# Splitting the second product around the first one, with the two row tiles exchanging PSUM banks

## The chip, the core and the metric

The kernel runs on one core of a Trainium2 chip. The metric is the device time of one execution in microseconds (us); lower is better. The engines are TensorE (PE in the profile; its weight loads are shown apart as PEld), VectorE (DVE), ScalarE (ACT), GpSimd (POOL) and SyncE (SP, which issues DMAs). They run side by side and meet through semaphores.

## The reference, cut to what matters

```python
def sm(a, b):
    s = scale * (a @ b.transpose(0, 2, 1))
    s = s - s.max(-1, keepdims=True)
    e = np.exp(s)
    return e / (e.sum(-1, keepdims=True) + 1e-09)
x = sm(q, agents) @ (sm(agents, k) @ v)      # q, k, v: (2, 12480, 128), agents: (2, 49, 128)
x = x.reshape(24960, 128)
h = x @ w_in                                 # 128 -> 2048
g = np.maximum(h, 0.0) + alpha * np.minimum(h, 0.0)
out = g @ w_out                              # 2048 -> 128
```

## The kernel before

The kernel first does the agent attention of batch 0 and folds the result with `w_in` into a table `sab` of 49 agents x 2048 features. After that a main loop runs over 24,960 tokens. It takes them in 52 groups of 480 (`GT`), and each group in 8 steps (`NM`) of 256 features: 416 steps. Two groups share one softmax of the queries, so what else happens in the loop repeats every 16 steps, 26 times. The agent attention of batch 1 (`kb`, `v`, `e`, `kl`, `av` in the names) is done in pieces between the steps of batch 0.

Values are split into a high and a low part to keep precision, so each product is three matmul jobs: low x high, high x low, high x high.

A **first product** `g1(s)` gives `h`, 256 features of 480 tokens, from the query softmax `qmh`, `qml` and `sab`. 49 agents fit into 64 rows, so the PE array is used as two row tiles of 64 rows: the upper tile computes one block of 128 features, the lower tile the other, and each writes a PSUM bank of its own. That is three pairs of matmuls. ScalarE then writes `rh`, the high part of max(h, 0), and VectorE writes `rl`, the rest. `h` has two buffers, so `g1(s + 2)` may start only when `rh` and `rl` of step `s` have been taken from `h`.

A **second product** `g2(s)` multiplies `rh` and `rl` with the two parts of `w_out` (`wh`, `wl`, scaled by 1 - alpha) and adds into `acc`. Here each block of 128 features is cut into its upper and lower 64 rows; the upper row tile adds into bank 0 of `acc`, the lower into bank 1. Six jobs of two matmuls are six pairs: four that need `rh` alone, and then two that need `rl`. After the eighth step three more matmuls add the linear part of the activation (`zh`, `zl`), one on the upper tile and two on the lower; ScalarE and VectorE add the two banks into `os`, and the result is transposed, scaled and stored.

The order of work is written out: instructions of an engine stand in the order in which the Python code issues them, and a planner (`at`, `pre`, `fit`, `hold`) places the other work in the steps. One step issues: the work in `first` (copies of earlier results out of PSUM), `g1(s + 2)`, the planned work of the step (some of it matmuls: `lg`, `qsum`, `kl`, `av`), and `g2(s)`. The other groups of PSUM (`pair_tile`) take turns with `acc`. The functions that the change touches:

Of the kernel before, what the change touches and what calls it, by code (L numbers as in the profile page):

```python
# [31 lines left out]
def kernel(  # L32
# [11 lines left out]
    nc = tc.nc  # L44
# [7 lines left out]
    GT = 480  # L52
# [10 lines left out]
    NM = NF // 2  # L63
# [14 lines left out]
    TILES = ((0, HALF), (HALF, P))  # L78
# [3 lines left out]
    def pair_tile(name, i=None):  # L82

        i = (step[0] // NM + 1) % 2 if i is None else i
        return late[i].tile([P, 2, 512], F32, tag="x", name=name)
# [22 lines left out]
    wh = const.tile([P, NF, D], F32R, name="wh")  # L108
    wl = const.tile([P, NF, D], F32R, name="wl")
# [684 lines left out]
    hh, rr, oo = {}, {}, {}  # L794
# [17 lines left out]
        )  # L812
        rr[s] = (rh, rl)

    def g2(s):
        g, m = divmod(s, NM)
        w = st[g // NG]
        if m == 0:
            oo[g] = pair_tile(f"acc{g}", g % 2)
        acc = oo[g]  # L820
        rh, rl = rr.pop(s)
        jobs = [(wl, rh, 0), (wh, rh, 0), (wl, rh, 1), (wh, rh, 1), (wh, rl, 0), (wh, rl, 1)]
        for n, (a, x, u) in enumerate(jobs):
            for i, (r0, r1) in enumerate(TILES):
                nc.tensor.matmul(  # L825
                    acc[:, i, 0:GT], lhsT=a[r0:r1, 2 * m + u, :], rhs=x[r0:r1, u, :],
                    start=m == 0 and n == 0, stop=False,
                )
        if m == NM - 1:
            mh, ml = gq.pop(("M", g))  # L830
            for i, a, x in ((0, "zh", mh), (1, "zl", mh), (1, "zh", ml)):
                r0, r1 = TILES[i]
                nc.tensor.matmul(  # L833
                    acc[:, i, 0:GT], lhsT=w[a][r0:r1, :], rhs=x[r0:r1, :],
                    start=False, stop=x is ml or i == 0,
                )
            t = p1m.tile([P, GT], F32, tag="os", name=f"os{g}")
            nc.scalar.copy(out=t, in_=acc[:, 0, 0:GT])  # L838
            nc.vector.tensor_tensor(out=t, in0=acc[:, 1, 0:GT], in1=t, op=ALU.add)  # L839
            oo[g] = t  # L840
# [28 lines left out]
    with tc.manual_schedule():  # L869
# [30 lines left out]
        s = 0  # L900
        for c, (lo, hi) in enumerate(spans):
# [4 lines left out]
            s = max(s, hi + 5)  # L906
# [18 lines left out]
        for n in range(8):  # L925
            load, ops = (load_win, narrow_win) if n < 4 else (load_wo, narrow_wo)
            s = int(SLAB_FIRST + n * SLAB_STEP)
# [59 lines left out]
        def fit(s, **costs):  # L987

            while any(load.get((e, s), 0.0) + c > ROOM[e] for e, c in costs.items()):
                s += 1  # L990
            for e, c in costs.items():
                use(s, e, c)
            return s
# [3 lines left out]
        def hold(s):  # L997

            while s in busy or s + 1 in busy or s % NM in (0, 1, NM - 1):
                s += 1  # L1000
            busy.update((s, s + 1))
            return s
# [28 lines left out]
        for b in range(1, B):  # L1031
# [4 lines left out]
            s = base + 9  # L1036
            done, used = {}, {}
            for c, (lo, hi) in enumerate([*parts[:-1], (NU - 3, NU - 1), (NU - 1, NU)]):
                us = tuple(range(lo, hi))
                for u in us:  # L1040
                    s = fit(max(s, done.get(u - 3, 0) + 1), dve=0.57)
# [12 lines left out]
            s = t_max + 1  # L1054
# [3 lines left out]
            for lo, hi in parts:  # L1058
                us = list(range(lo, hi))
                t_av = s  # L1060
                for u in us:
                    s = fit(s, dve=0.3)
# [16 lines left out]
            s = t_av + 2  # L1079
# [3 lines left out]
            for f in lead:  # L1083
                s = hold(s)
                at(s, f)
                s += 2
            s = hold(s)
# [5 lines left out]
        for s in range(NS):  # L1093
            step[0] = s
            for f, a in first.pop(s, ()):
                f(*a)
            if s + 2 < NS:
                g1(s + 2)
            for f, a in plan.pop(s, ()):
                f(*a)  # L1100
            g2(s)
        for s in sorted(plan):
            for f, a in plan[s]:
                f(*a)
# [30 lines left out]
```

## Time and profile before

| | |
|---|---|
| median of 3 runs | 1071.53 us (1068.31 to 1077.67) |
| the profiled execution: its own time | 1069.83 us |
| its span in the trace | 1068.0 us |
| PE busy, of the span | 1027.9 us, 96% |
| VectorE busy | 821.9 us, 77% |
| ScalarE busy | 629.5 us, 59% |

The profile is of one execution. Its span is what the trace covers; 1.8 us of the execution's time lie outside it. A line number such as L803 is that of the kernel's file. Matmul rows overlap: a row begins when the matmul begins, and its duration holds a tail in which the next one already runs, so the pace of PE is read from the distance between starts.

### The profile page before, as it was taken

The page shows a single profiled execution, that of the slowest core. Times are in us where ns is not written, and L with a number is a line of the kernel's source. Part 1 is how long each engine was busy: PE and PEld are TensorE (multiplying, and loading weights), DVE is VectorE, ACT ScalarE, POOL GpSimd, SP SyncE. Part 2 cuts the span into 40 slices and gives each one's busy share as a digit, 9 for nine tenths or more (in the row PEclk, how much of TensorE's full clock was granted, in tenths as well). Part 3 has the DMA queues.
Part 4 walks back from the last instruction along what each step waited for, and adds up shares of the span by engine and source line. Part 5 has one row for each costly group of instructions (what it writes and reads, how often), then busy time and mean ns, then how long its engine had stood idle before and what let it go on. Part 6 is the DMA issues. An engine that isn't in the chain of part 4 may idle for free.

```text
span 1068.0 us, 22363 instructions
## 1 busy us (share of the span) xinstructions
PE 1027.9 (96%) x9252; PEld 918.1 (86%) x9252; DVE 821.9 (77%) x1057; ACT 629.5 (59%) x805; POOL 111.7 (10%) x138
## 2 busy tenths in 40 slices
PE   7978999999999999999999999999999999999997
PEld 6865888888888888888877899998999989989997
DVE  6776588778778799989767777787778777786775
ACT  4454456556556577777555666566556665665553
POOL 3231110110110110110011011101110111001100
PEclk9889999999999999999999999999999999999999
DMA  8943041432331233233021022111211021202011
GB/s 295 287 96 49 4 76 30 68 60 37 61 59 28 55 71 77 69 79 62 11 39 30 16 33 38 30 20 29 37 30 33 16 38 30 39 11 38 11 20 29
DMA packets 295046, 57.23 MB, mean 54 GB/s; under 512 B 265567, under 2 KB 292769, under 8 KB 294945
## 3 DMA queue, kind: packets, MB, share of 16 engines
q1 hardware_dynamic: 293953, 55.69, 25.9%
q8 instruction: 72, 1.18, 0.5%
q14 instruction: 29, 0.24, 0.1%
q10 hardware_dynamic: 992, 0.12, 0.1%
HBM read 42.59 MB, written 12.78 MB: 52 GB/s over the span
## 4 chain that ended last, share of the span: by engine, by line
PE 63%; DVE 19%; ACT 12%; issue 4%; DMA 1%; SPq 0%; DVEq 0%; ACTq 0%
PE acc L825 33%; PE h L803 19%; DVE rl L810 8%; ACT rh L809 5%; PE lg L722 3%; ACT qs L749 3%; ACT qmh L744 3%; PE kl L379 2%; DVE qs L740 2%; PE av L567 1%; ACT os L838 1%; DVE qml L753 1%; DVE mx L418 1%; PE av L534 1%; DVE ql L712 1%
## 5 line engine op out<-in xcount | busy, mean ns | idle before, releaser
L810 DVE SCALAR_TENSOR_TENSOR rl<-h,rh 128x960 fp32r<-128x960 f32 x416 | 476.1, 1151 | 193.9 <-ACT rh L809 191.4
L809 ACT ACTIVATE rh<-h 128x960 fp32r<-128x960 f32 x416 | 402.4, 973 | 318.0 <-PE h L803 305.4
L803 PE MATMUL h<-qmh,sab 64*128 64x480 f32 x1664 | 378.0, 384 | 13.4 <-DVE rl L810 12.0
L825 PE MATMUL acc<-rh,wl 64*128 64x480 f32 x1664 | 374.8, 380 | 0.0
L825 PE MATMUL acc<-rh,wh 64*128 64x480 f32 x1664 | 371.9, 377 | 0.0
L825 PE MATMUL acc<-rl,wh 64*128 64x480 f32 x1664 | 294.2, 378 | 0.0
L803 PEld LDWEIGHTS h<-qmh,sab 64*128 64x128 f32 x1664 | 216.7, 184 | 49.5 <-DVE rl L810 32.6
L825 PEld LDWEIGHTS acc<-rh,wl 64*128 64x128 f32 x1664 | 217.8, 184 | 17.2 <-issue 3.4
L825 PEld LDWEIGHTS acc<-rh,wh 64*128 64x128 f32 x1664 | 218.3, 184 | 12.8
L825 PEld LDWEIGHTS acc<-rl,wh 64*128 64x128 f32 x1664 | 200.1, 184 | 14.2
L803 PE MATMUL h<-qml,sab 64*128 64x480 f32 x832 | 200.8, 378 | 0.0
L735 POOL PARTITION_ALL_REDUCE qm<-qs x26 | 79.2, 3045 | 761.0 <-ACT qs L730 694.3
L803 PEld LDWEIGHTS h<-qml,sab 64*128 64x128 f32 x832 | 111.5, 185 | 5.6
L379 PEld LDWEIGHTS kl<-ag,kt 64*128 64x128 f32 (+2 forms) x588 | 49.2, 192 | 2.6 <-issue 0.7
L379 PE MATMUL kl<-ag,kt 64*128 64x49 f32 (+2 forms) x588 | 50.0, 272 | 0.2 <-ACT kt L351 0.2
L839 DVE TENSOR_TENSOR os<-acc,os 128x480 f32<-128x480 f32 x52 | 33.6, 647 | 19.9 <-ACT os L838 19.8
L838 ACT COPY os<-acc 128x480 f32<-128x480 f32 x52 | 28.7, 551 | 23.3 <-PE acc L833 23.3
L707 ACT CAST qh<-qt 128x960 fp32r<-128x960 f32 x26 | 25.9, 998 | 16.1 <-DVE qt L700 16.1
L844 DVE STREAM_TRANSPOSE ot<-os 128x480 f32<-128x480 f32 x52 | 34.0, 653 | 0.0
L849 DVE TENSOR_TENSOR ot<-ot,qr 128x480 f32<-128x480 f32 x52 | 33.7, 648 | 0.1
L744 ACT ACTIVATE qmh<-qs,padb 128x960 fp32r<-128x960 f32 x26 | 28.5, 1098 | 7.7 <-DVE qs L740 7.7
L730 ACT COPY qs<-lg 128x960 f32<-128x960 f32 x26 | 25.0, 960 | 13.6 <-PE lg L722 13.6
(143 smaller groups left out, 856.6 us busy)
## 6 DMA issues: line engine op xcount, KB each, us to landing
qin<-in_q_dram SPq DMA_DIRECT2D x208, 60.0 KB, 2.2
out_dram<-ot SPq DMA_DIRECT2D x206, 60.0 KB, 1.9
v<-in_v_dram SPq DMA_DIRECT2D x12, 512.0 KB, 7.4
kb<-in_k_dram SPq DMA_DIRECT2D x96, 64.0 KB, 2.2
v<-in_v_dram SPq DMA_DIRECT2D x24, 256.0 KB, 2.8
k<-in_k_dram SPq DMA_DIRECT2D x11, 512.0 KB, 8.2
win<-in_moe_w_in_dram SPq DMA_DIRECT2D x4, 512.0 KB, 7.9
wo<-in_moe_w_out_dram SPq DMA_DIRECT2D x4, 512.0 KB, 9.5
```

The costliest lines, as they stand in the source:

```text
L379: nc.tensor.matmul(d[0:rows, c : c + NA], lhsT=kt[r0:r1, n * rows : (n + 1) * rows], rhs=st[b]["ag"][r0:r1, 0:NA], start=True, stop=True,)
L722: nc.tensor.matmul(t[:, i, 0:GT], lhsT=a[r0:r1, h].rearrange("p d a -> p (d a)"), rhs=x[r0:r1, h, :], start=n == 0, stop=n == len(jobs) - 1,)
L735: nc.gpsimd.partition_all_reduce(flat(t), flat(gq["s", k]), P, ReduceOp.max)
L744: nc.scalar.activation(out=m, in_=gq["s", k], func=AF.Exp, bias=padb, scale=SCALE)
L803: nc.tensor.matmul(h[:, u, 0:GT], lhsT=w[a][r0:r1, f0 : f0 + P], rhs=x[r0:r1, :], start=n == 0, stop=n == 2,)
L809: nc.scalar.activation(out=rh, in_=h[:, :, 0:GT], func=AF.Relu)
L810: nc.vector.scalar_tensor_tensor(out=rl, in0=h[:, :, 0:GT], scalar=0.0, in1=rh, op0=ALU.max, op1=ALU.subtract)
L825: nc.tensor.matmul(acc[:, i, 0:GT], lhsT=a[r0:r1, 2 * m + u, :], rhs=x[r0:r1, u, :], start=m == 0 and n == 0, stop=False,)
L838: nc.scalar.copy(out=t, in_=acc[:, 0, 0:GT])
L839: nc.vector.tensor_tensor(out=t, in0=acc[:, 1, 0:GT], in1=t, op=ALU.add)
L844: nc.vector.transpose(out=t.rearrange("p t i -> p (t i)"), in_=oo.pop(g))
L849: nc.vector.tensor_tensor(out=t, in0=t, in1=gq.pop(("r", g)).to_broadcast([P, TB, 32]), op=ALU.mult)
```

## The change

`g2` gets a second argument and is called twice in a step. `g2(s, 0)` does the three jobs of the first block of 128 features (`wl` x `rh`, `wh` x `rh`, `wh` x `rl`) ahead of `g1(s + 2)`; `g2(s, 1)` does the three jobs of the second block after the planned work. The number of matmuls is the same. `turn` says which row tile goes first and adds into bank 0: between part 0 and part 1 of a step the tiles change places, between a step and the next they don't. The last matmul of part 0 increments a new semaphore `turned` when it is done (the drain of the code leaves no instruction of its own in the built program), and the first matmul of part 1 waits for it. The instructions of VectorE, ScalarE, GpSimd and SyncE stand in the same order as before.

```diff
-    def g2(s):
+    turned = tc.alloc_semaphore("turned")
+
+    def g2(s, part):
         g, m = divmod(s, NM)
         w = st[g // NG]
-        if m == 0:
+        if m == 0 and part == 0:
             oo[g] = pair_tile(f"acc{g}", g % 2)
         acc = oo[g]
-        rh, rl = rr.pop(s)
-        jobs = [(wl, rh, 0), (wh, rh, 0), (wl, rh, 1), (wh, rh, 1), (wh, rl, 0), (wh, rl, 1)]
-        for n, (a, x, u) in enumerate(jobs):
-            for i, (r0, r1) in enumerate(TILES):
-                nc.tensor.matmul(
-                    acc[:, i, 0:GT], lhsT=a[r0:r1, 2 * m + u, :], rhs=x[r0:r1, u, :],
-                    start=m == 0 and n == 0, stop=False,
-                )
-        if m == NM - 1:
+        rh, rl = rr[s] if part == 0 else rr.pop(s)
+        turn = (s + part) % 2
+        if part == 1:
+            nc.tensor.wait_ge(turned, s + 1)
+        for n, (a, x) in enumerate(((wl, rh), (wh, rh), (wh, rl))):
+            for i in range(2):
+                r0, r1 = TILES[(i + turn) % 2]
+                ins = nc.tensor.matmul(
+                    acc[:, i, 0:GT], lhsT=a[r0:r1, 2 * m + part, :], rhs=x[r0:r1, part, :],
+                    start=m == 0 and part == 0 and n == 0, stop=False,
+                )
+        if part == 0:
+            nc.tensor.drain(fusable=True).then_inc(turned, 1)
+        if m == NM - 1 and part == 1:
...
+            g2(s, 0)
             if s + 2 < NS:
                 g1(s + 2)
             for f, a in plan.pop(s, ()):
                 f(*a)
-            g2(s)
+            g2(s, 1)
```

One step on PE before, late in the main loop (names end in buffer numbers; the bracket names the engine whose semaphore is waited for, and `PE_49` is PE's own):

```order
L803 MATMUL h_13459<-qmh_13120,sab_6982 128x480 [waits DVE_49]
L803 MATMUL h_13459<-qmh_13120,sab_6982 128x480
L803 MATMUL h_13459<-qml_13153,sab_6982 128x480 x2
L803 MATMUL h_13459<-qmh_13120,sab_6982 128x480 x2
L825 MATMUL acc_13375<-rh_13418,wl 128x480 [waits Activation_49]
L825 MATMUL acc_13375<-rh_13418,wl 128x480
L825 MATMUL acc_13375<-rh_13418,wh 128x480 x2
L825 MATMUL acc_13375<-rh_13418,wl 128x480 x2
L825 MATMUL acc_13375<-rh_13418,wh 128x480 x2
L825 MATMUL acc_13375<-rl_13419,wh 128x480 x4
L803 MATMUL h_13482<-qmh_13120,sab_6982 128x480 [waits DVE_49]
```

A step of the same kind on PE after the change:

```order
L830 MATMUL acc_13451<-rh_13522,wl 128x480 [waits Activation_49]
L830 MATMUL acc_13451<-rh_13522,wl 128x480
L830 MATMUL acc_13451<-rh_13522,wh 128x480 x2
L830 MATMUL acc_13451<-rl_13523,wh 128x480 [waits DVE_49]
L830 MATMUL acc_13451<-rl_13523,wh 128x480
L803 MATMUL h_13582<-qmh_12950,sab_7337 128x480 [waits PE_49]
L803 MATMUL h_13582<-qmh_12950,sab_7337 128x480
L803 MATMUL h_13582<-qml_12986,sab_7337 128x480 x2
L803 MATMUL h_13582<-qmh_12950,sab_7337 128x480 x2
L830 MATMUL acc_13451<-rh_13522,wl 128x480 [waits turned]
L830 MATMUL acc_13451<-rh_13522,wl 128x480
L830 MATMUL acc_13451<-rh_13522,wh 128x480 x2
```

The wait for VectorE has moved from the first matmul of `h` to the fifth matmul of the step, behind two pairs that need `rh`; `h` now begins three pairs into the step and carries a wait for an older matmul of PE itself; and part 1 begins with the wait for `turned`.

The end of the program on PE after the change, where no `h` is left to compute:

```order
L830 MATMUL acc_14374<-rh_14533,wl 128x480 [waits Activation_49]
L830 MATMUL acc_14374<-rh_14533,wl 128x480
L830 MATMUL acc_14374<-rh_14533,wh 128x480 x2
L830 MATMUL acc_14374<-rl_14534,wh 128x480 [waits DVE_49]
L830 MATMUL acc_14374<-rl_14534,wh 128x480
L830 MATMUL acc_14374<-rh_14533,wl 128x480 [waits turned]
L830 MATMUL acc_14374<-rh_14533,wl 128x480
L830 MATMUL acc_14374<-rh_14533,wh 128x480 x2
```

In the last two steps the two parts stand next to each other, so part 1 waits for the matmul directly ahead of it.

## Rows read from the trace of the kernel before

**Rows 1.** The page: busy time of each engine, share of the span, instructions.

```profile
PE 1027.9 (96%) x9252; PEld 918.1 (86%) x9252; DVE 821.9 (77%) x1057; ACT 629.5 (59%) x805; POOL 111.7 (10%) x138
```

**Rows 2.** The page: the chain that ended last, by engine and line.

```profile
PE 63%; DVE 19%; ACT 12%; issue 4%; DMA 1%; SPq 0%; DVEq 0%; ACTq 0%
PE acc L825 33%; PE h L803 19%; DVE rl L810 8%; ACT rh L809 5%; PE lg L722 3%; ACT qs L749 3%; ACT qmh L744 3%; PE kl L379 2%; DVE qs L740 2%; PE av L567 1%; ACT os L838 1%; DVE qml L753 1%; DVE mx L418 1%; PE av L534 1%; DVE ql L712 1%
```

**Rows 3.** Timeline of PE: start, duration (us), engine, line, instruction, count.

```profile
668.12 0.38 PE L803 MATMUL h<-qml,sab 64*128 64x480 f32 x2
668.33 0.38 PE L803 MATMUL h<-qmh,sab 64*128 64x480 f32 x2
668.54 0.39 PE L764 MATMUL qsum<-qml,ones 64*128 64x480 f32 x2
...
668.98 0.39 PE L825 MATMUL acc<-rh,wl 64*128 64x480 f32 x2
...
670.27 0.41 PE L803 MATMUL h<-qmh,sab 64*128 64x480 f32 x2
...
670.93 0.41 PE L825 MATMUL acc<-rh,wl 64*128 64x480 f32 x2
```

**Rows 4.** Waits of PE's weight loads, whole span: us in total, times, longest.

```profile
PEld h L803 <- DVE rl L810: 32.6, 48, 1.1
```

**Rows 5.** The same view, 100 to 600 us.

```profile
PEld h L803 <- DVE rl L810: 21.9, 36, 1.1
```

**Rows 6.** The same view, 600 to 1000 us.

```profile
PEld h L803 <- DVE rl L810: 9.8, 11, 0.9
```

**Rows 7.** Timeline of all engines, 659 to 669 us; bracket: idle before, releaser.

```profile
659.67 0.97 ACT L809 ACTIVATE rh<-h 128x960 fp32r<-128x960 f32 x1 [1.00 <-PE h L803]
...
660.68 1.16 DVE L810 SCALAR_TENSOR_TENSOR rl<-h,rh 128x960 fp32r<-128x960 f32 x1 [0.81 <-ACT rh L809]
...
661.76 1.15 DVE L740 TENSOR_TENSOR qs<-qs,qm 128x960 f32<-128x960 f32 x1
...
662.93 1.10 ACT L744 ACTIVATE qmh<-qs,padb 128x960 fp32r<-128x960 f32 x1 [0.31 <-DVE qs L740]
...
663.64 0.38 PE L803 MATMUL h<-qmh,sab 64*128 64x480 f32 x1
...
664.13 1.10 ACT L749 ACTIVATE qs<-qs,padb 128x960 f32<-128x960 f32 x1
...
665.13 0.54 ACT L838 COPY os<-acc 128x480 f32<-128x480 f32 x1
...
665.57 1.84 ACT L809 ACTIVATE rh<-h 128x960 fp32r<-128x960 f32 x2
...
666.58 1.16 DVE L810 SCALAR_TENSOR_TENSOR rl<-h,rh 128x960 fp32r<-128x960 f32 x1 [0.22 <-ACT rh L809]
...
667.79 0.19 PEld L803 LDWEIGHTS h<-qmh,sab 64*128 64x128 f32 x2 [0.89 <-DVE rl L810]
667.79 0.49 PE L803 MATMUL h<-qmh,sab 64*128 64x480 f32 x2 [0.48 <-DVE rl L810]
...
668.75 0.98 ACT L809 ACTIVATE rh<-h 128x960 fp32r<-128x960 f32 x1 [1.34 <-PE h L803]
```

**Rows 8.** Timeline of all engines, 674 to 676.5 us.

```profile
674.89 1.12 DVE L810 SCALAR_TENSOR_TENSOR rl<-h,rh 128x960 fp32r<-128x960 f32 x1
...
675.74 0.64 PE L825 MATMUL acc<-rl,wh 64*128 64x480 f32 x4
...
676.06 0.19 PEld L803 LDWEIGHTS h<-qmh,sab 64*128 64x128 f32 x2
```

**Rows 9.** Timeline of PE, 534.9 to 536.7 us, end of a group.

```profile
535.36 0.38 PE L833 MATMUL acc<-qmh,zh 64*128 64x480 f32 x1
535.38 0.37 PE L833 MATMUL acc<-qmh,zl 64*128 64x480 f32 x1
535.59 0.38 PE L803 MATMUL h<-qmh,sab 64*128 64x480 f32 x1
535.59 0.38 PE L833 MATMUL acc<-qml,zh 64*128 64x480 f32 x1
...
535.81 0.59 PE L803 MATMUL h<-qmh,sab 64*128 64x480 f32 x2
```

## The prediction

> **What bounds the kernel now.** I began with the page's busy times: PE 96%, VectorE 77%, ScalarE 59% [rows 1]. The chain that ended last agrees: 63% of it is PE, and 19% and 12% are VectorE and ScalarE, mostly the lines that make `rl` and `rh` [rows 2]. So PE sets the pace, with places at which it waits for the other two. The timeline of PE gives the pace where nothing waits: from the first `acc` pair of a step at 668.98 to that of the next at 670.93 stand nine pairs in 1.95 us, **0.217 us a pair** [rows 3], and 416 steps of nine pairs are 812 us. No matmul is removed, so the pace can only change through waits and through the order of the row tiles.
>
> The view of PE's waits shows one that matters in the main loop: the first weight load of `h` waiting for VectorE's `rl`, 32.6 us in 48 places [rows 4]. 36 of them (21.9 us) lie between 100 and 600 us, where the second batch's attention is mixed in [rows 5], and 11 (9.8 us) in 600 to 1000 us [rows 6]. So about 33 us, 3% of the time, is the most that a better place for this wait could give.
>
> The timeline shows how it comes about [rows 7]. At 659.67 ScalarE, idle for 1.00 us, begins `rh` as soon as PE has finished an `h`; VectorE, idle for 0.81, makes `rl` at 660.68; then come the subtraction of the query softmax (661.76), two exponentials (662.93, 664.13), the copy of `acc` (665.13), `rh` again (665.57), `rl` (666.58), and at 667.79 PE's weight load, which stood idle for 0.89 us. From an `h` of PE back to PE the links follow one another closely. The question is what the change does to the two ends of such a chain.
>
> **The change part by part.** *Where `rl` is needed.* Take the beginning of a step on PE as zero. Before, `rl(s)` was needed at 0, since `h` of step s + 2 came first; now two pairs that need only `rh` come ahead of it, so it is needed 2 x 0.217 = 0.43 us later. That is the gain, in each place where `rl` is late.
>
> *Where `h` is produced.* Before, `h(s + 2)` was complete after three pairs of the step; now three pairs of the second product go ahead, and it is complete after six: 0.65 us later. ScalarE and VectorE start from `h`, and their own order is unchanged. A chain that starts from an `h` ends 0.65 us later while its end is needed only 0.43 us later. Counted in pairs: between the end of `g1(s)` and the need for `rl(s)` stood fifteen pairs, `g2`, `g1` and `g2` (6 + 3 + 6); now it is fourteen, part 1, a part 0, `g1`, a part 1 and the two pairs (3 + 3 + 3 + 3 + 2). **One pair of slack, 0.217 us, is lost** each time that a chain reaches from an `h` to a late `rl`, after which PE has taken that delay over and the next chain starts afresh.
>
> `rh(s)` is now needed at the beginning of the step, six pairs earlier than before by the same count, but it is done at least one `rl` (1.16 us [rows 7]) ahead of the `rl` for which PE used to wait at that point, and the 0.65 us by which `h` is later leave 0.5 us of that. Nothing.
>
> *How often.* In 600 to 1000 us a cycle of sixteen steps lasts some 37 us: 11 waits [rows 6] are one a cycle. In the same cycle there is a second place that the waits don't list: an `rl` that ends at 674.89 + 1.12 = 676.01, and the weight load of `h` at 676.06, where the last four matmuls before it began at 675.74 and a free load would have stood at about 675.96 [rows 8]. It has no slack to give away. So two places a cycle. Earlier there are 36 waits in some 13.5 cycles [rows 5], 2.7 a cycle; they come in runs of two or three neighbouring steps, and within a run the delay is paid once, so two a cycle there too. 26 cycles x 2 x 0.217 = 11.3 us is the upper end of this term; with one place a cycle it is 26 x 0.217 = 5.6 us. Where a tenth of a microsecond of slack is left it takes part of the pair. I take 40 places: **+8.7 us**.
>
> *The new wait.* `turned` is incremented when the last matmul of part 0 is done. How long a result takes to be seen elsewhere is in the trace: the last pair of `h` begins at 668.33 and ScalarE, idle, begins at 668.75: 0.42 us [rows 3, 7]. Between that matmul and the first of part 1 stand the three pairs of `g1`; a weight load is issued when the matmul before it on its tile starts, so it is wanted three pairs, 0.65 us, after. 0.23 us are to spare, more where planned matmuls stand between; the same row tile ends part 0 and begins part 1, so that a lead of one tile over the other doesn't use it up. What is queued behind it on PE is part 1 and the next step; nobody waits for that but the next `h`. Cost taken: 0. The wait of a PE weight load on a PE matmul so close ahead is not in the trace, so the other bound is that the load isn't prefetched: after a wait the next pair starts 668.12 - 667.79 = 0.33 us on instead of 0.217 [rows 3, 7], 0.11 more, 416 x 0.11 = 46 us. In the last two steps nothing stands between the parts: 0.42 for the signal and 0.11 for the bare load less the 0.217 that the pair takes anyway, 0.31 each, **+0.6 us**.
>
> The other wait on `h`, for an older PE matmul, is for one of two steps back: 0.
>
> *The exchange of tiles.* Once a step a matmul now follows one of its own row tile. The rows have this at each group's end: `zl` at 535.38 and the next `zh` matmul are both on the lower tile and start 535.59 - 535.38 = 0.21 us apart, while the upper tile goes on to `h` at 535.59 [rows 9]. That is the ordinary pace: 0. The Trainium skill, "TensorE: Matmul & The Clock Gate", part 3 (the mechanism), says otherwise: a weight load overlaps a running matmul only when their row groups differ; by that each exchange would bare a load. This trace disagrees in these rows; by the page the sum would be the 1125 us of the last rival below.
>
> Sum against the profiled execution's own time: 1069.8 + 8.7 + 0.6 = **1079 us**, 0.9% above it and 0.7% above the median of the runs.
>
> **The rivals.** *The two pairs are a gain (faster).* If the late end of a chain doesn't move when `h` comes later, PE keeps the two pairs: 48 x 0.43 = 21 us less, 1049. For it: at 665.57 the `rh` that PE's wait hung on began 1.5 us after its own `h` could have been read, because ScalarE was busy with the exponentials (the last `h` matmul began at 663.64, and 0.42 on is 664.06 [rows 7]); that `h` could have come 0.65 us later for nothing. Against it: those exponentials themselves hang on an `h` of two steps before, on which both engines had idled [rows 7], and that one moves too. It decides where a chain starts from something other than PE, a DMA or the reduction on GpSimd. In between lie times from 1049 to 1065.
>
> *The new wait is paid each step (slower).* If the signal from PE to PE takes longer than the 0.65 us, or the load behind it is not prefetched, each step pays: 46 us for the bare load, 1069.8 + 46 + 9 = 1125; each further 0.1 us is 42 us. It decides from 0.65 us of latency on; the 0.42 us speaks against it. A smaller cost of 10 to 40 ns a step (a signal that ties up the issue of the next instructions) gives 1083 to 1096.
>
> *Each exchange bares a weight load (slower).* 416 x 0.11 = 46 us as well, 1125 with the lost slack; the lower tile's ordinary 0.21 us speaks against it [rows 9]. It decides if a load on the tile that is computing is held back.
>
> **How the numbers follow.** The forecast (lost slack, 1072 to 1086) gets 0.60, the gain 0.17, the new wait 0.17 with half of that at the small cost, the bare load at each exchange 0.06. Predicted: 1079. The range goes from 1058, which takes in part of the gain, to 1104, which takes in the small costs of the wait; it leaves out the full gain and the full price of the two slower rivals. About 1%, 10.7 us, is what a measurement of this kernel tells from no change. The forecast lies at 9.3 us, just inside it: of its 0.60 I count 0.40 as no change and 0.20 as slower. Of the gain 0.12 is faster and 0.05 no change; the slower rivals hold 0.23, of which 0.02 lie within the bound. Summed: faster 0.12, same 0.47, slower 0.41.
>
> **What would show it.** In the changed profile the weight loads that wait for `rl` would be those of `acc`, with more of them than 48 and a sum above 32.6 us, in about two places a cycle; the pace of nine pairs where nothing waits would still be 1.95 us; the first `acc` load of part 1 would start with the last `h` pair, with no idle time. If it starts later, the new wait is paid. If same-tile neighbours start 0.33 us apart, the bare load is. If PE's idle time falls below 32.6 us, the chains don't move with `h` and the forecast fails in its main step.

## The result, and the profile after

The changed kernel took 1087.09 us (median of 4 runs, 1078.07 to 1089.68) against 1072.68 us of the kernel before (1068.31 to 1077.67): a ratio of 1.0117 with a 95% interval of 1.0069 to 1.0166. It is slower by about 1.2%, inside the forecast range and 8 us above the forecast. The profiled execution took 1084.75 us, 14.95 us more than that of before.

The page of the changed kernel, busy times and the chain that ended last:

```profile
PE 1042.2 (96%) x9252; PEld 927.3 (86%) x9252; DVE 824.5 (76%) x1057; ACT 629.9 (58%) x805; POOL 111.8 (10%) x138
...
PE 63%; DVE 18%; ACT 12%; issue 4%; DMA 1%; SPq 1%; DVEq 0%; ACTq 0%
```

The shares are those of [rows 1, 2], and no engine has become a new bound. PE's busy time is 14.3 us longer with the same 9252 matmuls, which is no extra work: where PE waits, the row ahead of the wait runs its tail of some 0.16 us past the usual next start, the row right behind it lasts 0.49 us instead of 0.38 (679.73 below), and at the lower clock of the start a row lasts 0.60 us (e7). So the busy times don't tell where the time went. The waits do; first the view of the waits of PE's weight loads, then that of its matmuls (us in total, times, longest), whole span:

```profile
PEld acc L830 <- DVE rl L810: 35.2, 54, 1.0
PEld acc L830 <- ACT rh L809: 9.9, 22, 1.2
PEld acc L830 <- ACT os L845: 4.3, 3, 1.5
...
PEld acc L830 <- PE acc L830: 0.9, 2, 0.5
```

```profile
PE acc L830 <- DVE rl L810: 13.8, 32, 0.6
PE acc L830 <- DVE x L577: 4.9, 5, 1.1
```

The wait of `h` for `rl` [rows 4] has become one of `acc`, and grown from 32.6 us in 48 places to 35.2 in 54. Three waits are new: for `rh`, and two that the prediction doesn't speak of, for `os` and `x`. They are not to be added up, since a weight load and its matmul can wait for the same thing. The wait for another `acc` matmul, which is how `turned` shows, is there in two places alone, the last two steps.

The timeline of all engines, 677.9 to 680.9 us, shows the place in the cycle that answers to [rows 7]:

```profile
677.51 1.84 ACT L809 ACTIVATE rh<-h 128x960 fp32r<-128x960 f32 x2
...
678.52 1.16 DVE L810 SCALAR_TENSOR_TENSOR rl<-h,rh 128x960 fp32r<-128x960 f32 x1 [0.22 <-ACT rh L809]
678.53 0.19 PEld L830 LDWEIGHTS acc<-rh,wl 64*128 64x128 f32 x2 [0.38 <-ACT rh L809]
...
679.73 0.18 PEld L830 LDWEIGHTS acc<-rl,wh 64*128 64x128 f32 x2 [0.90 <-DVE rl L810]
679.73 0.49 PE L830 MATMUL acc<-rl,wh 64*128 64x480 f32 x2 [0.49 <-DVE rl L810]
```

PE waits twice in one step: first for `rh`, then, two pairs on, for the `rl` that VectorE makes from it. The second wait alone is as long as the whole one before (0.89 us [rows 7]). The second place, which the waits of before didn't list [rows 8], is now one of them (same view, 687.0 to 690.5 us):

```profile
687.04 1.12 DVE L810 SCALAR_TENSOR_TENSOR rl<-h,rh 128x960 fp32r<-128x960 f32 x1
...
688.21 0.18 PEld L830 LDWEIGHTS acc<-rl,wh 64*128 64x128 f32 x2 [0.32 <-DVE rl L810]
```

Where nothing waits, the pace and the beginning of part 1 are as forecast (680.5 to 683.2 us):

```profile
680.92 0.19 PEld L830 LDWEIGHTS acc<-rh,wl 64*128 64x128 f32 x2
681.13 0.39 PE L830 MATMUL acc<-rh,wl 64*128 64x480 f32 x2
...
682.88 0.38 PE L803 MATMUL h<-qmh,sab 64*128 64x480 f32 x2
682.89 0.19 PEld L830 LDWEIGHTS acc<-rh,wl 64*128 64x128 f32 x2
683.10 0.39 PE L830 MATMUL acc<-rh,wl 64*128 64x480 f32 x2
```

From the first `acc` pair of one part 1 at 681.13 to that of the next at 683.10 stand nine pairs in 1.97 us (1.95 before [rows 3]). Its first load starts at 682.89, 0.01 us after the last pair of `h`, with no idle time: the wait for `turned` is over by then. Both loads of the pair start there, while a matmul runs on either tile, so a load doesn't wait for its own tile to be free.

**Stretch by stretch.** The whole time is a blunt measure here. Up to the `h` of step 1, which is issued ahead of the loop, no kernel differs, and yet its last pair began anywhere from 90.8 to 103.6 us in the thirteen profiles. So I count from it. The last `h` pair of each of the 416 steps is found in PE's timeline, and its start times cut the loop: from `h` of step 1 to that of step 16, to 104 (before the second batch's attention), to 208 (after it), to 415 (the last), and to the end. "Cycle" is the median of sixteen steps from step 240 on. All are us of the profiled execution.

| kernel | slack of `rl`, pairs | 1–16 | 16–104 | 104–208 | 208–415 | tail | 1 to end | cycle |
|---|---|---|---|---|---|---|---|---|
| before | 15 | 45.1 | 215.6 | 250.1 | 450.0 | 11.2 | 972.1 | 34.94 |
| after | 14 | 47.3 | 217.8 | 255.6 | 453.2 | 11.2 | 985.1 | 35.22 |
| e1, split only | 14 | 47.6 | 217.8 | 255.6 | 453.2 | 10.7 | 984.8 | 35.22 |
| e2, exchange only | 15 | 45.1 | 215.6 | 250.1 | 450.2 | 12.1 | 973.1 | 34.94 |
| e6, closing matmul | 15 | 45.1 | 215.6 | 250.2 | 450.1 | 11.2 | 972.2 | 34.95 |
| e4, two ahead | 15 | 47.1 | 215.4 | 253.3 | 448.9 | 10.8 | 975.4 | 34.84 |
| e9, `rl` second | 13 | 47.8 | 220.0 | 257.1 | 458.3 | 10.9 | 994.1 | 35.65 |
| e10, `rl` first | 12 | 46.4 | 222.1 | 258.6 | 463.2 | 11.1 | 1001.4 | 36.09 |
| e3, group start | 12 to 17 | 45.1 | 217.7 | 253.2 | 457.6 | 10.7 | 984.2 | 35.58 |
| e5, all ahead | 13 | 49.2 | 219.0 | 259.7 | 453.9 | 11.4 | 993.2 | 35.25 |
| e7, start as before | 14 | 45.1 | 218.0 | 255.6 | 453.3 | 10.7 | 982.7 | 35.22 |
| e8, behind, groups | 13 to 17 | 45.1 | 215.3 | 250.8 | 452.8 | 10.8 | 974.7 | 35.16 |
| e11, behind, late | 15 | 45.1 | 215.4 | 250.8 | 448.9 | 10.8 | 971.0 | 34.84 |

After minus before is 13.0 us: 2.2 at the start, 2.2 to step 104, 5.5 to step 208, 3.2 to step 415, nothing in the tail. One caution: in the split order `h` comes three pairs later within its step, so 0.65 us of the start's difference is only the cut (0.43 with two pairs ahead). The tail has to be that much shorter for it: e1's is 0.55 us shorter than that of before, the changed kernel's is not, so its tail hides a loss. The cuts between are all shifted alike.

### The profile page after: what moved, and what is told of

Same layout as the page of the kernel before. It is cut to its first block, busy times and chain, and to the rows that moved or that the text cites. A ratio compares the mean times of both kernels' runs of the same rounds, so it can differ in the third digit from the quotient of the medians.

```text
span 1083.0 us, 22363 instructions
## 1 busy us (share of the span) xinstructions
PE 1042.2 (96%) x9252; PEld 927.3 (86%) x9252; DVE 824.5 (76%) x1057; ACT 629.9 (58%) x805; POOL 111.8 (10%) x138
## 4 chain that ended last, share of the span: by engine, by line
PE 63%; DVE 18%; ACT 12%; issue 4%; DMA 1%; SPq 1%; DVEq 0%; ACTq 0%
PE acc L830 33%; PE h L803 18%; DVE rl L810 8%; ACT rh L809 5%; PE kl L379 4%; PE lg L722 3%; ACT qs L749 2%; ACT qmh L744 2%; DVE qs L740 2%; PE ktp L347 1%; PE av L534 1%; DVE ql L712 1%; ACT os L845 1%; DVE qml L753 1%; PE a_ps L628 1%
## 5 line engine op out<-in xcount | busy, mean ns | idle before, releaser
L830 PE MATMUL acc<-rl,wh 64*128 64x480 f32 x1664 | 377.5, 385 | 14.3 <-DVE rl L810 13.8
L830 PE MATMUL acc<-rh,wl 64*128 64x480 f32 x1664 | 380.3, 385 | 5.0 <-DVE x L577 4.9
L803 PE MATMUL h<-qmh,sab 64*128 64x480 f32 x1664 | 355.0, 378 | 0.0
L830 PEld LDWEIGHTS acc<-rl,wh 64*128 64x128 f32 x1664 | 197.2, 184 | 48.8 <-DVE rl L810 35.2
L830 PEld LDWEIGHTS acc<-rh,wl 64*128 64x128 f32 x1664 | 201.9, 184 | 32.3 <-ACT rh L809 9.9
L830 PEld LDWEIGHTS acc<-rh,wh 64*128 64x128 f32 x1664 | 202.7, 185 | 11.7
L803 PEld LDWEIGHTS h<-qmh,sab 64*128 64x128 f32 x1664 | 197.2, 185 | 13.8 <-DVE sab L630 1.5
L803 PE MATMUL h<-qml,sab 64*128 64x480 f32 x832 | 185.0, 378 | 0.0
L803 PEld LDWEIGHTS h<-qml,sab 64*128 64x128 f32 x832 | 99.4, 185 | 6.3
L379 PEld LDWEIGHTS kl<-ag,kt 64*128 64x128 f32 (+2 forms) x588 | 55.0, 205 | 2.5 <-issue 0.6
L379 PE MATMUL kl<-ag,kt 64*128 64x49 f32 (+2 forms) x588 | 55.4, 284 | 0.2 <-ACT kt L351 0.2
L707 ACT CAST qh<-qt 128x960 fp32r<-128x960 f32 x26 | 26.0, 1000 | 15.7 <-DVE qt L700 15.6
```

Of the source, the lines that this page charges most:

```text
L379: nc.tensor.matmul(d[0:rows, c : c + NA], lhsT=kt[r0:r1, n * rows : (n + 1) * rows], rhs=st[b]["ag"][r0:r1, 0:NA], start=True, stop=True,)
L803: nc.tensor.matmul(h[:, u, 0:GT], lhsT=w[a][r0:r1, f0 : f0 + P], rhs=x[r0:r1, :], start=n == 0, stop=n == 2,)
L830: ins = nc.tensor.matmul(acc[:, i, 0:GT], lhsT=a[r0:r1, 2 * m + part, :], rhs=x[r0:r1, part, :], start=m == 0 and part == 0 and n == 0, st ...
```

## The experiments

The theory after the result was that of the prediction: the split takes a pair of slack from `rl`. The rivals were that the wait for `turned` or the exchange of tiles costs, or that the division itself does.

**e1 and e2: one half of the change each.** e1 has the split, but neither the exchange nor the wait; e2 has the old order with the exchange and the wait.

```
# e1, against after
-            nc.tensor.wait_ge(turned, s + 1)
...
-                r0, r1 = TILES[(i + turn) % 2]
+                r0, r1 = TILES[i]
...
-            nc.tensor.drain(fusable=True).then_inc(turned, 1)
# e2, against before
+        turn = (m + 1) % 2
+        if m:
+            nc.tensor.wait_ge(turned, s)
...
+                r0, r1 = TILES[(i + turn) % 2]
...
+        nc.tensor.drain(fusable=True).then_inc(turned, 1)
```

> The split without the exchange of tiles and without the wait for turned: the upper tile always adds into bank 0. If the order of the work is what costs (my theory), this is as slow as the changed kernel: 1087 us, some 14 above the kernel before, with the same 35.2 us for a cycle of sixteen late steps (34.93 before) and the same waits of the first acc matmul of a group for the addition of av. If the exchange and its wait cost (the rival), it is back near 1073 us. If the exchange itself helps a little, as the free steps of the changed kernel suggest (1.969 us from h to h against 1.974 to 1.980), it is up to 4 us above the changed kernel.

> The order of before; the tiles change places from one step to the next, and the first acc matmul of a step waits for the last of the step before, with the same three pairs of h between as in the changed kernel. By my theory the wait is covered (0.42 us of latency against 0.65 us): 1073 us as before, or some 3 us less if the exchange is what quickens the free steps. If the wait or the exchange costs 0.1 us a step, 42 us more: 1115 us; if they are what the changed kernel lost, 1087 us.

e1: 1080.63 us, ratio to before 1.0109 [1.0069, 1.0149], against 1.0117 with the whole change. e2: 1069.25 us, ratio 0.999 [0.9954, 1.0025]. In the table e1 is the changed kernel in every stretch but the tail, and e2 is the kernel before. e2's waits of the weight loads begin as [rows 4] do, to the digit:

```profile
PEld h L803 <- DVE rl L810: 32.6, 48, 1.1
```

So the split makes the whole loss; the exchange of the tiles and the wait neither cost nor bring anything in the loop. Only where nothing stands between the signal and the wait do they show. In e2's tail (timeline of PE, 1065.7 to 1068.6 us) two steps in a row have no `h` between them:

```profile
1065.72 0.64 PE L831 MATMUL acc<-rl,wh 64*128 64x480 f32 x3
1066.52 0.49 PE L831 MATMUL acc<-rh,wl 64*128 64x480 f32 x2 [0.15 <-PE acc L831]
...
1067.46 0.63 PE L831 MATMUL acc<-rl,wh 64*128 64x480 f32 x4
1068.24 0.48 PE L831 MATMUL acc<-rh,wl 64*128 64x480 f32 x2 [0.15 <-PE acc L831]
```

The four matmuls from 1067.46 are two pairs, so without a wait the next would begin 0.43 us later, at 1067.89; it begins at 1068.24, 0.35 us later than that. That is the price of the wait uncovered in e2, whose trace has 337 more semaphore instructions on PE's queue; the changed kernel's has none more and pays 0.22 us, and whether that makes the difference was not tried. e2's tail is 0.8 us longer than that of before (12.06 against 11.22).

**e4: the lost pair given back.** Two pairs, those of `rh`, stand ahead of the first product, the other four behind it, so that `rl` is again needed by `h` and fifteen pairs stand between.

```
+        jobs = [(wl, rh, 0), (wh, rh, 0), (wl, rh, 1), (wh, rh, 1), (wh, rl, 0), (wh, rl, 1)]
+        jobs = jobs[:2] if part == 0 else jobs[2:]
```

> Two pairs that need only rh ahead of g1, the other four, rl among them, behind it; no exchange, no wait. Fifteen pairs again from the end of g1 to the need for rl, but acc still begins ahead of g1. By my theory the late cycles are those of before (34.9 us), and what remains of the loss is the wait of a new group's first acc matmul for the addition of av, some 5 us between steps 104 and 208, and what the beginning of the loop lost: 1078 to 1081 us. If the lost pair of slack is not what the late cycles pay, they stay at 35.2 us and the time at 1087 us.

1075.25 us, ratio 1.0024 [0.9991, 1.0057]. The stretches 16 to 104 and 208 to 415 fall below those of before (215.4 and 448.9) and the cycle to 34.84 us. So it is not the division that costs there. `rl` is needed two pairs later than before and `h` comes two pairs later, and nothing is gained at the two late places: the chain does move with `h`. What remains is at the start (47.1) and in the attention stretch (253.3, against 250.1): the lost slack is not all.

**e6: the lead of a row tile.** At the end of a group three matmuls close the sum, two of them on the lower tile [rows 9]. In e6 the third alternates between the tiles from group to group.

```
+            k = g % 2
-            for i, a, x in ((0, "zh", mh), (1, "zl", mh), (1, "zh", ml)):
+            for i, a, x in ((0, "zh", mh), (1, "zl", mh), (k, "zh", ml)):
```

> The kernel before, with the third of the three closing matmuls of a group on the lower tile for odd groups and on the upper tile for even ones, so that each tile has 26 extra matmuls instead of 52 on the lower. If the lower tile sets the pace and the lead of the upper one is kept, up to 26 x 0.217 = 5.6 us less: 1067 us. If the two tiles are brought level by PE's waits anyway, nothing: 1073 us.

1073.36 us, ratio 0.9993 [0.9962, 1.0025], all stretches as before: one step becomes shorter and the next wait gives the same back. A lead of one tile over the other is worth nothing here, with or without an exchange.

**e9 and e10: the slack as a dose.** e1 with another order within the part ahead of the first product: the pair that needs `rl` second, or first. Nothing else moves, so that thirteen and twelve pairs are left.

```
# e9
+        order = ((wl, rh), (wh, rl), (wh, rh)) if part == 0 else ((wl, rh), (wh, rh), (wh, rl))
# e10
+        order = ((wh, rl), (wl, rh), (wh, rh)) if part == 0 else ((wl, rh), (wh, rh), (wh, rl))
```

> The split in two parts everywhere, without the exchange and the wait, but in the part ahead of the first product the pair that needs rl comes second instead of third. Nothing else moves, the copies of acc included. Between the end of g1(s) and the need for rl(s) stand thirteen pairs, with the split as changed fourteen, and fifteen where four pairs stand behind. If the loss of the late cycle is the lost slack, each of its two places grows by a further pair of 0.217 us: the late cycle goes from 34.84 (fifteen) and 35.22 (fourteen) to about 35.65 us, and over 26 cycles the whole time is some 11 us above the split's. The rival, that the pairs ahead of the first product cost by something else (the division, the later h alone), leaves the cycle at 35.2 us.

> The same with the pair that needs rl first in the part ahead of the first product: twelve pairs of slack. By the lost slack the late cycle comes to about 36.1 us, or more where a third place in the cycle runs out of slack too; the whole time is some 22 us above the split's. The rival leaves the cycle at 35.2 us.

e9: 1096.92 us, ratio 1.0222 [1.0154, 1.0291]. e10: 1100.61 us, ratio 1.0258 [1.0178, 1.0339]. The cycles are 35.65 and 36.09 us, as written down for the slack. From `h` of step 1 to the end e9 is 9.3 us and e10 16.6 us above e1, less than the 11 and 22 that were expected of the whole time. The two places, read from the starts of `h` in the cycle (medians of ten cycles, us from one step's `h` to the next):

| slack, pairs | 15 (e4) | 14 (after) | 13 (e9) | 12 (e10) |
|---|---|---|---|---|
| first place | 2.76 | 2.96 | 3.18 | 3.41 |
| second place | 1.97 | 2.15 | 2.37 | 2.59 |
| cycle | 34.84 | 35.22 | 35.65 | 36.09 |

Each pair costs 0.18 to 0.23 us at each of the two places; the other fourteen steps don't move by more than 0.03 us. From the view of the waits of PE's weight loads, from `h` of step 224 to that of step 415, e4 first:

```profile
PEld h L803 <- DVE rl L810: 9.8, 11, 0.9
PEld acc L826 <- ACT rh L809: 2.1, 11, 0.2
```

The changed kernel:

```profile
PEld acc L830 <- DVE rl L810: 13.1, 21, 0.9
PEld acc L830 <- ACT rh L809: 4.1, 11, 0.4
```

e10:

```profile
PEld acc L826 <- DVE rl L810: 25.0, 21, 1.6
```

With fifteen pairs there is one wait for `rl` a cycle, with fourteen and with twelve two. In e10 the wait for `rh` is gone and the cycle is the longest of all: at the late places, the wait for `rl` would have taken the time that PE waits for `rh`.

**e5: all six pairs ahead.** The whole second product first, undivided, then the first product and the planned work. By the count thirteen pairs.

```
+            g2(s)
             if s + 2 < NS:
                 g1(s + 2)
...
-            g2(s)
```

> The whole second product ahead of the first product and of the planned work, not split. Counted in pairs, thirteen stand between the end of g1(s) and the need for rl(s), instead of fourteen with the split and fifteen before. If slack is what is lost, the late cycle of sixteen steps goes on from 34.93 (fifteen) and 35.22 (fourteen) to 35.6 to 35.7 us (thirteen), by a further pair at each of its two places: 0.45 and 0.39 us above before instead of 0.24 and 0.17. If it is the division into two parts that costs, the cycle goes back to 34.9, since nothing is divided here. The waits of acc for rl then come to more than 35.3 us in total by the first theory. The waits at the groups' starts should be longer than with the split too, since the same matmuls stand ahead of g1; the whole time by slack 1085 to 1095 us, by division about 1073.

1093.11 us, ratio 1.0192 [1.0145, 1.0239]. The whole time is what the slack gave, but by luck: what it lost more lies in the start (49.2) and in the attention stretch (259.7, where PE waits 8.1 us for `x`), and the cycle is 35.25 us and not 35.6: of the two places only the second moved (2.35 us from `h` to `h`, 0.38 above before), the first stayed at 2.69. This kernel also moves the copies of `acc` at a group's end ahead of the next `rh`, and at the first place such a copy stands in the chain, just ahead of `rh` [rows 7]. That would shorten it, but I have not isolated it; e5 is no clean dose, which is why e9 and e10 were run.

**e3: the groups' first steps.** The waits for `os` and `x` come at the beginning of a group of eight steps, where the first matmul of a new `acc` needs its PSUM bank. Timeline of the changed kernel, 422.5 to 428.5 us:

```profile
424.51 1.15 DVE L810 SCALAR_TENSOR_TENSOR rl<-h,rh 128x960 fp32r<-128x960 f32 x1
...
425.58 0.68 DVE L493 TENSOR_TENSOR v<-v,v 128x512 fp32r<-128x512 f32 x1
...
426.18 0.69 DVE L577 TENSOR_TENSOR x<-av,x 98x516 f32<-98x516 f32 x1
...
426.98 0.22 PEld L830 LDWEIGHTS acc<-rh,wl 64*128 64x128 f32 x2 [1.47 <-ACT os L845]
427.01 0.48 PE L830 MATMUL acc<-rh,wl 64*128 64x480 f32 x2 [1.10 <-DVE x L577]
```

The bank held `av` of the second batch's attention, which VectorE adds up at L577, behind an `rl` and a split of `v`. The first `acc` pair used to stand behind `g1` and the planned work of its step; now it comes ahead of both and waits 1.47 us. e3 puts both parts of such a step back behind them, with the split elsewhere.

```
+            if s % NM:
                 g2(s, 0)
...
+            if s % NM == 0:
+                g2(s, 0)
             g2(s, 1)
```

> The split without the exchange and without the wait, but in the first step of each group of eight (s a multiple of 8) both parts stand behind the first product and the planned work, as before. In the stretch of the second batch's attention (from h of step 104 to h of step 208) the kernel with the split everywhere takes 255.6 us and the kernel before 250.1. If most of that is the new waits of the group's first matmul of acc for VectorE's x (L577, 4.8 us in 5 places) and for ScalarE's os (4.3 us in 3 places), these two waits fall below 1 us each and the stretch takes 249 to 252 us; some of the waits for rl that had vanished come back. If the stretch is longer because of the lost pair of slack alone, it stays above 254. The order also changes the slack of rl: seventeen pairs in the third step of a group, twelve in the first, fourteen in the others, so the late cycle of sixteen steps, 35.22 with the split everywhere and 34.93 before, may lie anywhere between 34.6 (the third step's place gains two pairs) and 35.6 us (the first step's twelve pairs are too few). Whole time by the first theory some 5 us below the split everywhere.

1083.74 us, ratio 1.0086 [1.0052, 1.012]. The attention stretch falls from 255.6 to 253.2 us, below the 254 at which slack alone was to leave it, but not to 249 to 252; the waits fall to 1.3 us (`x`) and 2.2 us (`os`), not below 1. The cycle rises to 35.58: where a group's first step has only twelve pairs of slack, a new late place appears, in that step of every second group. That price is paid in the cycles from step 208 on; from 16 to 104 the same order costs nothing (217.7 against 217.8), and in the attention stretch no such place shows in the distances from `h` to `h`. So the groups' first steps are worth 2.4 us here, and the rest of the 5.5 has another cause.

**e7: the first sixteen steps.** The split from step 16 on, the old order ahead of it.

```
+            if s >= 16:
                 g2(s, 0)
...
+            if s < 16:
+                g2(s, 0)
             g2(s, 1)
```

> The split without the exchange and the wait, but the first sixteen steps in the order of before (first product, planned work, both parts). From the first matmul of acc to h of step 16 the kernel before takes 40.9 us and the kernel with the split 46.2. If that difference comes from the split part standing ahead of the planned work in the first steps (the turning of the input weights waits longer, and TensorE's granted clock drops behind it), this stretch goes back to 40.9 us and the rest stays as with the split: 217.8 for the steps 16 to 104, 255.6 to 208, 35.2 for a late cycle; the whole time is then about 5 us below the split everywhere. If the first steps only take up a delay that any start of the split order costs, the 5 us move behind step 16, and 16 to 104 takes about 222 us.

1080.65 us, ratio 1.0086 [1.0045, 1.0127]. From the first matmul of `acc` it took 40.9 us to `h` of step 16, as written, and the rest stayed. But that yardstick flatters: in the split order the first `acc` pairs come ahead of the transposes that turn the input weights, so the count begins earlier. From `h` of step 1 the split costs 2.2 us (after) and e7 takes it all back; of the 2.2, 0.65 is the cut, as said, so some 1.6 us are real. To the end of the program e7 is 2.1 us shorter than e1, not the 5 that were expected. Most of it is one event. PE's timeline of the changed kernel, 105.8 to 112.5 us, and the granted clock (third number from the end, then DMA share and GB/s) in two windows:

```profile
105.91 0.37 PE L803 MATMUL h<-qmh,sab 64*128 64x480 f32 x2
108.50 1.06 PE L662 MATMUL turn<-ident,win 128*128 128x128 f32 x8 [2.22 <-DVE lin L666]
...
110.45 0.61 PE L830 MATMUL acc<-rh,wl 64*128 64x480 f32 x2
110.85 0.61 PE L830 MATMUL acc<-rh,wh 64*128 64x480 f32 x2
```

```profile
105.00:110.00 5.00, 2.78 (x24) 2.09 (x22) 3.41 (x4) 2.42 (x3) 0.00 (x0) 1.00 0.00 0
110.00:115.00 5.00, 5.00 (x34) 4.09 (x31) 1.91 (x3) 0.97 (x1) 0.00 (x0) 0.66 0.00 0
```

After 2.22 us without work, PE's pairs come 0.40 us apart instead of 0.217: it runs at 1.2 GHz instead of 2.4. At 0.66 of the clock over 5 us, it lost 0.34 x 5 = 1.7 us, by estimate. In e7 PE waits 1.55 us at the same place and the clock stays at 1.00:

```profile
110.00:115.00 5.00, 3.45 (x30) 2.67 (x28) 4.49 (x5) 1.19 (x2) 0.00 (x0) 1.00 0.00 0
```

Seven kernels have the old order in their first step and wait 1.1 to 1.6 us there: none drops. Six have pairs ahead and wait 2.0 to 2.6 us: five drop (after, e1, e4, e5, e9); e10, with 2.2 us, doesn't, and what decided there stays open. Each is one profiled execution. e10 also gives the price from the other side: it has a pair of slack less than e9, and yet its start is 1.3 us shorter (46.44 us against 47.77).

The longer idle time is the split's. PE waits for VectorE's scaling of the weights (L666), the end of a chain over VectorE and ScalarE that starts from the `h` of step 2: its `rl`, a transpose of the queries (L700), their cast (L707), `rh` and `rl` of step 3, the scaling. In the changed kernel:

```profile
101.82 1.16 DVE L810 SCALAR_TENSOR_TENSOR rl<-h,rh 128x960 fp32r<-128x960 f32 x1 [0.80 <-ACT rh L809]
...
104.69 1.00 ACT L707 CAST qh<-qt 128x960 fp32r<-128x960 f32 x1 [2.90 <-DVE qt L700]
...
106.59 1.16 DVE L810 SCALAR_TENSOR_TENSOR rl<-h,rh 128x960 fp32r<-128x960 f32 x1 [1.93 <-ACT rh L809]
107.67 0.68 DVE L666 TENSOR_TENSOR lin<-turn,alp 128x512 f32<-128x512 f32 x1
```

From the `rl` of step 2 to PE's transposes it is 6.68 us here and before (99.27 to 105.95). What is later is its `h`, which follows the `h` of step 1 after 2.56 us instead of 1.90, and the idle time has grown by the same. PE waits twice for such transposes, before:

```profile
99.17 1.10 PE L662 MATMUL turn<-ident,win 128*128 128x128 f32 x8 [0.95 <-DVE sab L630]
...
105.95 1.06 PE L662 MATMUL turn<-ident,win 128*128 128x128 f32 x8 [1.55 <-DVE lin L666]
```

and the first of these waits has shrunk to 0.30 us in the changed kernel, where three pairs now fill it. PE doesn't idle longer in all; it idles longer in one piece.

**e8 and e11: the causes taken away together.** e8 is e4 with the old order in the first sixteen steps and in each group's first step; e11 keeps the old order in the groups' first steps below step 208 alone.

```
# e8
+            if s >= 16 and s % NM:
                 g2(s, 0)
...
+            if s < 16 or s % NM == 0:
+                g2(s, 0)
# e11
+            if s >= 16 and (s % NM or s >= 208):
...
+            if s < 16 or (s % NM == 0 and s < 208):
```

> Two matmul pairs of the second product, those that need rh of the first half alone, ahead of the first product and four behind, with the order of before in the first sixteen steps and in the first step of each group. It takes away all three causes that the earlier runs point to: fifteen pairs of slack for rl are there again, a group's first acc matmul stands where it stood, and so do the first steps. By them each stretch comes to that of before or below it: 40.9 us to h of step 16, 215 to 216 to step 104, 250 to 252 to step 208, and a late cycle of 34.4 to 34.9 us (seventeen pairs in a group's third step, where one of the cycle's two waits for rl lies); the whole time equals that of before, or is up to 10 us below it. The rival: thirteen pairs for rl in a group's first step are too few, and the late cycle stays above 35.0 us.

> Two pairs ahead of the first product and four behind it, with the order of before in the first sixteen steps and in the first step of each group below step 208 alone; from step 208 on all steps have the two pairs ahead. If the causes add up by place, the stretches are those measured one by one: 40.9 us to h of step 16, 215.3 to step 104, 250.8 to step 208, 34.84 for a late cycle and 414.0 for steps 224 to 415; from the first acc matmul to the end 966.6 us against 967.9 of before, a difference of 0.1% that the whole time can't show. If the third run's longer late cycle (35.17 us) did not come from the groups' first steps, it stays at 35.2.

e8: 1072.73 us, ratio 0.9996 [0.9962, 1.0031]. Its cycle is 35.16 us, the rival's: thirteen pairs in a group's first step are too few. ("The third run" in the second text is e8.) e11: 1069.79 us, ratio 0.9985 [0.9948, 1.0021]; from the first `acc` matmul to the end 966.7 us, with 966.6 expected, every stretch as measured one by one. The kernel to hold it against is e4. In its attention stretch the waits at the groups' starts shrink from e4's 3.8 and 3.7 us to 0.6 and 1.7 (views of PE's matmuls, then of its weight loads; e4 first):

```profile
PE acc L826 <- DVE x L577: 3.8, 5, 0.9
PE acc L826 <- DVE x L577: 0.6, 3, 0.2
```

```profile
PEld acc L826 <- ACT os L839: 3.7, 3, 1.2
PEld acc L826 <- ACT os L839: 1.7, 3, 0.6
```

250.8 us stand against e4's 253.3: 2.5 us for the groups' first steps. In e1, with the third pair ahead, these waits were longer still, 4.8 and 4.3 us. Taken step by step, 1.4 of the 2.2 us by which e1's attention stretch exceeds e4's lie in the distances to the `h` that is issued in a group's first step, seven of them 0.15 to 0.23 us longer, and only 0.8 in the others, where `rl` is late; e9 against e1, where the place of `rl` alone moves, adds nothing there (0.05 us) and 1.5 in the others. So the lost pair was paid there mostly by the chains that free the bank. e11 is the fastest of all by the stretches, 1.1 us below the kernel before; the whole time can't tell it from that.

## Why the prediction was right, and what it missed

- **The number alone would not have shown it.** 1087 us also lies in the 1083 to 1096 of the rival that the new wait ties up each step for 10 to 40 ns. It is e1 and e2 that tell the two apart. Of the loss itself, 14.4 us by the medians, 9.3 was forecast; it lies beyond the 10.7 us up to which the prediction counted "no change", the case that it had given the most.
- **The lost pair of slack: right, its size a little too large.** +8.7 us was forecast for `rl`. e1 against e4, the same order but for that pair, gives 2.4 (16 to 104) + 2.3 (104 to 208) + 4.3 (208 to 415) = 9.0 us; but 1.4 of what the attention stretch lost is that of the groups' first steps, which leaves 7.6 for `rl`. Two places a cycle, 0.217 us each, was the working: 0.20 and 0.18 were measured from fifteen to fourteen pairs, and 0.22 and 0.22 from fourteen to thirteen. It is the one step whose dose was tested. The 40 places were a choice between 26 and 52, not a count.
- **"They come in runs … two a cycle there too": right ahead of the attention, too high in it.** From 16 to 104 ten places pay, two a cycle. The attention stretch lost 0.8 us to `rl` in 6.5 cycles, against 2.8 by two places a cycle; from fourteen pairs to twelve it loses 1.5 a pair. The "some 37 us" of a late cycle, too, are 34.9; the 11 waits are one a cycle all the same.
- **"`rh` … Nothing": right for the time of the late cycles, wrong for the waits.** PE does wait for `rh`, 22 times and 9.9 us. The step failed to see that; but in e10, where this wait is gone, the cycle is longer, because `rl` ends last. What the view of waits lists need not cost. For the rest of the loop this was not tried.
- **The new wait and the exchange, 0: right.** e1 differs from the changed kernel by no more than 0.3 us in any stretch ahead of the tail, and e2 from the kernel before by 0.2.
- **The last two steps, +0.6 us: right in kind.** In the changed kernel's tail the parts' first loads come 0.22 us late at two places. 0.31 each was forecast. The tail as a whole is 0.55 us longer than e1's, which has no wait; that it equals the tail of before is the cut's doing.
- **What is missing: the destination of a moved matmul.** The part-by-part account asked of the three pairs that move ahead which operands they need, `rh` and `rl`, and not which bank they write. In a group's first step that bank may still be held by `av` or by the copy of the last `acc`. e11 against e4 puts two of the pairs at 2.5 us, and e1 against e4 the third at 1.4: 3.9 us.
- **What is missing: the start of the loop.** Some 1.6 us, nearly all by the lower clock, where PE's idle time had grown from 1.55 to 2.22 us; nothing in the prediction speaks of those steps.
- **Not forecast, and a gain: free steps are quicker.** e11 has fifteen pairs as before, and its cycle is 0.10 us shorter, some 0.01 us in each of the free steps, 1.1 us from step 208 on. It comes with the split (e1, e4) and not with the exchange (e2); why was not tried.

The sum: 7.6 (`rl`) + 3.9 (banks) + 1.6 (start) + 0.4 (tail) - 0.7 (e11 against before, 16 to 415) = 12.8 of the 13.0 us measured between the same points; the rest of the 14.95 us is the 1.9 us by which this profile's loop happened to begin later. The terms of the loop are differences between one kernel and the next, so they have to add up; that they hold apart from one another is shown by e11, whose stretches were written down beforehand. With the two missing terms the forecast would have been some 1085, and "slower", not "no change", the likeliest case. The rival that two pairs are a gain fell in its own condition: the late chains do start from PE, at both places, for in e4 both `h` and the need for `rl` come two pairs later, and with the `h` alone a pair later (e1) each place grows by some 0.2 us.

## What to carry to other kernels

When a consumer's work is split around its producer's, count the distance in matmuls between what starts the chain and what needs its end, before and after; it is the difference of the two that counts, and here one matmul pair was worth 9 us, in the chains of `rl` and in those that free a bank. Of each instruction that moves earlier ask three things: when its operands are there, when its destination is free, and which idle time it leaves behind where it stood. Work that fills one wait can lengthen the next, and one long piece of idle time can cost more than two short ones, as at the start here. A wait whose signal comes three pairs earlier is free; what it orders was not where the time lay.

## What the runs showed of the hardware

- The order of the row tiles is free: changing once a step which tile goes first moved no stretch of the loop (e2, 0.2 us in 415 steps), and neither did taking away a lead of one tile (e6).
- A signal from PE to PE that nothing covers costs 0.35 us at e2's last steps, 0.22 in the changed kernel's; three pairs, 0.65 us, cover it.
- A weight load starts while a matmul runs on its own row tile: both loads of a pair at 682.89, both matmuls at 682.88 us in the changed kernel.
- A lower clock can follow a short idle time: after 2.22 us without work the pairs came 0.40 us apart instead of 0.217. At that place it followed in five of six kernels that idled 2.0 to 2.6 us (not in e10, 2.2 us) and in none of seven that idled 1.1 to 1.6.
- Up to the `h` of step 1 the same instructions took 90.8 to 103.6 us in thirteen profiles, while nearly all late cycles of one kernel lie within 0.2% of each other (before: 34.88 to 34.95 us). A change of 1% is better measured between two points in the loop than from beginning to end.
